# Spreading a global group's steps over other units, and moving the second merged pass, in a fused window-attention and feed-forward kernel

## The chip, the cores and the metric

The kernel runs on one core of a Trainium2 chip. The metric is the device time of one execution in microseconds. Its engines work side by side, each through its own instructions in order: TensorE (matmuls; PE in the profile, its weight loads PEld), VectorE (DVE), ScalarE (ACT), GpSimd (POOL) and SyncE (SP), which here only issues transfers.

## The reference

Eight batches with eight heads each. Every head has 512 local positions and 32 global ones, of 64 features. A local query attends to the 32 global keys and to local keys at most 32 positions away; a global query attends to all 544 keys. The result, 4608 rows of 512, goes through a feed-forward part: relu, square, scale and shift between two matrix products.

```python
s_g = scale * q_g @ k_all.T ; out_g = softmax(s_g) @ v_all
mask = abs(pos[:, None] - pos[None, :]) <= 32
s_l = concat([scale * q_l @ k_g.T, where(mask, scale * q_l @ k_l.T, -1e9)])
out_l = softmax(s_l) @ concat([v_g, v_l])
x = concat([out_g, out_l], axis=2)      # as (4608, 512)
r = maximum(x @ w_in, 0) ; out = (s * r * r + b) @ w_out
```

## The kernel before, in words

**Units and passes.** An attention unit j (0 to 127) is one head of one half (256 queries) of one batch: batch j // 16, half (j // 8) % 2, head j % 8. The feed-forward part has 17 tiles of 256 rows (the last holds the global rows), with eight passes m each, 136 in all; a pass multiplies one tile with a 256-wide slice of the first weights (`ffn_in`, 24 matmuls in the split precision that is used from pass 3 on), squares the result, and multiplies it with the matching slice of the second weights into two accumulators (`ffn_out`, twelve matmuls, six for each accumulator). Units 0 to 15 and passes 0 to 7 stand in a list written out by hand (PLAN). From pass 8 on the loop at the end (lines 753 to 826) puts one unit into each pass, from unit 16 on; in the passes of TWO_HEADS it puts two, here called merged passes: pass 10 holds units 18 and 19, pass 13 units 22 and 23. Unit 24 stands in pass 14, and from there on unit j in pass j - 10.

**The order.** For TensorE, ScalarE and VectorE the order of the program is the order of the engine's instructions (a manual schedule). SyncE's and GpSimd's order after the list is made by a planner. A usual pass goes: `split` of a unit two ahead (two casts on ScalarE, L236 and L238, and two subtractions on GpSimd, L237 and L239, which give keys and queries as a high and a low part); `begin`: the unit's score matmuls (L419, and L423 for the global queries) into the one score bank `ps_s` and the one bank `ps_g`, the masked scores with their maximum (`sm_scores`, VectorE L251), the global scores' copy (ScalarE L431) and addition (VectorE L437); `weigh`: two exponentials (L262), sums (L269, L270), two divides (L278); every fourth unit (j % 4 = 1) `values`: the value product of two pairs of units (L381), from the units j - 5 to j - 2, pair by pair; `ffn_in(m)`; `turned`: four copies into `two` (L458) and a transfer that transposes them (L464); on the last pass of a tile `x_split`, the cast of the next tile (L572) into the one buffer that `ffn_in` reads, and its low part (L576); `relu` (ScalarE L621); the joining of the unit before (`join`, ScalarE L472, which waits for the transposed data); `square` (VectorE L625); `g_high` (ScalarE L629) and `g_low` (VectorE L633); and last on TensorE `ffn_out(m - 1)`. After the last pass of a tile (in the pass behind it, called border in the code) two output copies follow on ScalarE (L660) with their transfers.

**Global groups.** A group (b, g) is the global queries of four heads of batch b. Its scores are complete after unit 16 b + 11 (g = 0) or 16 b + 15 (g = 1). Then come: its softmax (`g_softmax`, maximum on VectorE L480 and L481, exponential on ScalarE L486, sum and divide on VectorE L490 to L492), which stands at the end of a pass behind `g_low` (list `early`); copies of its five pieces into two 16-bit planes (`g_planes`, VectorE L529, list `planes_at`, behind `square`); a transposing transfer (L534); the joining of the pieces (`g_join`, ScalarE L541, list `joins_at`, behind the unit's `join`); the load of its values (`g_load`, L546); and its value product (`g_pv`, L554, list `gpv`, before `ffn_in`). Group 0 and 1 of batch 0 are transposed on TensorE instead (`g_turn`, L510, five matmuls, copied by `g_part`, L514). With s0 = 16 b + 12 + 4 g the softmax stands at unit s0, the planes at s0 + 1 (three) and s0 + 2 (two, with the transfer), the joinings at s0 + 3 (two pieces, and the load) and s0 + 4 (three), the value product at s0 + 5. Group (0, 1) has its softmax at unit 17 and its value product at unit 25.

**Splits ahead.** In a merged pass two units are split, so the loop makes up: the second unit's successor is split in the merged pass, and pass 17 (CATCH_UP) splits one more, from where on splits are two units ahead.

Of the kernel before, what the change touches and what calls it, by code (L numbers as in the profile page):

```python
# [22 lines left out]
P = 128  # L23
# [25 lines left out]
TWO_HEADS = (10, 13)  # L49
# [23 lines left out]
CATCH_UP = 17  # L73
# [8 lines left out]
def window_attention_then_ffn(ctx: ExitStack, tc: tile.TileContext, qd, qp, qg, kw, vw, vg, w_in, w_out, out):  # L82
# [433 lines left out]
    def g_transposes(b, g):  # L516
        for part in range(2):
            g_turn(b, g, part)
            g_part(b, g, part)
            yield  # L520

# [119 lines left out]
    def ffn_out(m, turn):  # L641
        t, pr = m // 8, m % 8
        g = gs_.pop(m)
        if pr == 0:
            oacc[t] = [ps.tile([P, DM], F32, tag=f"acc{i}", name=f"acc{t}_{i}") for i in range(2)]
        for i in range(2):
            next(turn, None)
            n = 0
            for k in range(2):
                f = 2 * pr + k  # L650
                for e, a in terms(m):
                    nc.tensor.matmul(  # L652
                        oacc[t][i], lhsT=as_used(m, g[:, a, k, i * P:(i + 1) * P]), rhs=weight(f, e)[:, 512:1024],
                        start=(pr == 0 and n == 0), stop=(pr == 7 and n == 5),
                    )
                    n += 1
        if pr == 7:
            for i in range(2):
# [22 lines left out]
    def run_max(j):  # L681
# [14 lines left out]
        "Fo": lambda m: ffn_out(m, iter(())),  # L696
# [16 lines left out]
    for b in range(B):  # L713
        for g in range(2):
            s0 = 16 * b + G_AT[g]
            first = int((b, g) == (0, 1))
            early[s0 + first].append(lambda b=b, g=g: g_softmax(b, g))
            if b < G_PE:
                turns[s0 + 3] = g_transposes(b, g)
                (joins_at if first else early)[s0 + 2 + 2 * first].append(lambda b=b, g=g: g_load(b, g))  # L720
            else:
                planes_at[s0 + 1].append(lambda b=b, g=g: g_planes(b, g, 0, 3))
                planes_at[s0 + 2].append(lambda b=b, g=g: (g_planes(b, g, 3, 5), g_turn_dma(b, g)))
                joins_at[s0 + 3].append(lambda b=b, g=g: (g_join(b, g, 0, 2), g_load(b, g)))
                joins_at[s0 + 4].append(lambda b=b, g=g: g_join(b, g, 2, 5))
            gpv[s0 + G_PV + 4 * first].append(lambda b=b, g=g: g_pv(b, g))
# [27 lines left out]
    for m in range(8, NM + 1):  # L754
# [7 lines left out]
        for i in heads:  # L762
            head_loads(i)
# [139 lines left out]
```

## Time and profile before

| | us |
|---|---|
| median of three runs | 969.67 (969.21 to 970.29) |
| the profiled execution | 969.21 |
| its span in the profile | 967.4 |
| TensorE busy in it | 934.8 (97%) |
| ScalarE, VectorE, GpSimd busy | 722.3, 664.3, 220.2 |

The span runs from the first instruction to the last. Busy time of TensorE counts matmuls from start to a modelled end, so a matmul that waits for its data between others can still count as busy; lost time is better seen in how long a stretch with known content takes. A row of the timeline gives start, duration, engine and line, and in brackets how long the engine had idled before and what ended that.

### The profile page before, as it was taken

The numbers are of one execution on the slowest core, as the hardware profiler recorded it, in microseconds if no ns is written. First come the engines' busy times: TensorE is split into PE (matmuls) and PEld (weight loads), VectorE is DVE, ScalarE is ACT, GpSimd is POOL, SyncE is SP. The second block draws the span as 40 slices with busy tenths as digits, with TensorE's granted clock in tenths as the row PEclk, the third lists the DMA queues.
The fourth block names the chain that finished last, engine by engine and source line by source line (L and its number), as shares of the span: only waits on it lengthen the run. The fifth ranks groups of instructions, "written<-read, shape, count | busy, mean of one in ns | idle before, by whom it ended". The sixth has DMA issues, their size and how long they took to land.

```text
span 967.4 us, 19993 instructions
## 1 busy us (share of the span) xinstructions
PE 934.8 (97%) x7258; PEld 832.1 (86%) x7258; DVE 664.3 (69%) x2058; ACT 722.3 (75%) x1514; POOL 220.2 (23%) x245
## 2 busy tenths in 40 slices
PE   7889899999999999999999999999999999999996
PEld 3658788898999989998999889998999999999995
DVE  5999777777768776776767676777768776752221
ACT  6999687788778887888778787878778887752321
POOL 1010233332333232323323232323323232100000
PEclk8999989999999999999999999999999999999999
DMA  9953344466455553466346554456345564232000
GB/s 318 384 190 100 104 110 104 127 141 143 112 111 143 126 135 95 121 144 152 86 116 141 123 138 97 116 144 163 84 110 143 140 126 106 62 72 73 22 1 23
DMA packets 195979, 119.68 MB, mean 124 GB/s; under 512 B 144168, under 2 KB 185128, under 8 KB 195880
## 3 DMA queue, kind: packets, MB, share of 16 engines
q1 hardware_dynamic: 190864, 109.28, 45.0%
q10 hardware_dynamic: 5016, 9.13, 2.7%
q8 instruction: 57, 0.93, 0.4%
q14 instruction: 42, 0.34, 0.1%
HBM read 74.98 MB, written 9.44 MB: 87 GB/s over the span
## 4 chain that ended last, share of the span: by engine, by line
PE 57%; DVE 18%; ACT 14%; DMA 5%; issue 4%; ACTq 1%; SPq 0%; POOL 0%; DVEq 0%; POOLq 0%
PE ps_h L613 25%; PE acc L652 23%; ACT sm L262 3%; PE ps_op L381 3%; DVE two L458 3%; PE ps_s L419 3%; DVE r L625 3%; DMA turned<-two 2%; DMA wst<-in_w_out 2%; ACT kq L236 2%; ACT g L629 2%; DVE wst L185 2%; ACT ptp L472 1%; DVE g L633 1%; DVE sm L278 1%
## 5 line engine op out<-in xcount | busy, mean ns | idle before, releaser
L613 PE MATMUL ps_h<-xs,wh 128*128 128x256 f32 x1584 | 288.8, 283 | 3.0 <-DVE r L625 2.8
L237 POOL TENSOR_TENSOR kq<-rk,kq 64x416 fp32r<-64x416 f32 x112 | 128.5, 1148 | 589.7 <-ACT kq L236 563.4
L652 PE MATMUL acc<-wh,g 128*128 128x512 f32 x792 | 249.1, 395 | 1.8 <-DVE g L633 1.4
L613 PEld LDWEIGHTS ps_h<-xs,wh 128*128 128x128 f32 x1584 | 243.5, 189 | 6.8 <-DVE r L625 2.9
L613 PE MATMUL ps_h<-xs,wl 128*128 128x256 f32 x792 | 220.0, 280 | 0.0
L633 DVE SCALAR_TENSOR_TENSOR g<-r,sb_t,g 128x512 fp32r<-128x512 f32 x133 | 100.5, 756 | 100.7 <-ACT g L629 100.7
L652 PEld LDWEIGHTS acc<-wh,g 128*128 128x128 f32 x792 | 142.8, 189 | 29.2 <-DVE g L633 3.0
L472 ACT COPY ptp<-turned 128x1024 int16<-128x1024 int16 x112 | 152.1, 1360 | 11.2 <-DMA turned<-two 11.0
L652 PE MATMUL acc<-wl,g 128*128 128x512 f32 x396 | 155.4, 392 | 0.0
L613 PEld LDWEIGHTS ps_h<-xs,wl 128*128 128x128 f32 x792 | 149.5, 189 | 0.1
L621 ACT ACTIVATE r<-ps_h 128x512 f32<-128x512 f32 x136 | 81.4, 599 | 89.4 <-PE ps_h L613 85.3
L625 DVE SCALAR_TENSOR_TENSOR r<-ps_h,sb_t,r 128x512 f32<-128x512 f32 x136 | 101.5, 747 | 56.4 <-ACT r L621 54.6
L629 ACT ACTIVATE g<-r,sb_t 128x512 fp32r<-128x512 f32 (+1 forms) x136 | 98.2, 722 | 50.8 <-DVE r L625 50.2
L262 ACT ACTIVATE sm<-sm,nm 128x224 f32<-128x224 f32 (+1 forms) x256 | 117.6, 461 | 6.2 <-DVE nm L251 4.6
L458 DVE COPY two<-sm 128x256 int16<-128x256 int16 x448 | 100.7, 288 | 8.7 <-DMA turned<-two 8.6
L613 PE MATMUL ps_h<-xs,w 128*128 128x256 f32 x816 | 102.8, 282 | 0.0
L652 PE MATMUL acc<-w,g 128*128 128x512 f32 x408 | 100.2, 393 | 0.2
L613 PEld LDWEIGHTS ps_h<-xs,w 128*128 128x128 f32 x816 | 98.1, 188 | 1.8
L652 PEld LDWEIGHTS acc<-wl,g 128*128 128x128 f32 x396 | 74.6, 188 | 16.6
L652 PEld LDWEIGHTS acc<-w,g 128*128 128x128 f32 x408 | 74.2, 188 | 15.8 <-DVE g L633 1.3
L239 POOL TENSOR_TENSOR kq<-rq,kq 128x256 fp32r<-128x256 f32 x112 | 83.9, 749 | 8.8
L419 PE MATMUL ps_s<-kq 128*128 128x192 f32 (+1 forms) x448 | 79.0, 266 | 5.3 <-POOL kq L237 5.1
(79 smaller groups left out, 1144.5 us busy)
## 6 DMA issues: line engine op xcount, KB each, us to landing
rvp<-in_vw SPq DMA_DIRECT2D x64, 256.0 KB
rq<-in_qd SPq DMA_DIRECT2D x112, 128.0 KB
rk<-in_kw SPq DMA_DIRECT2D x56, 208.0 KB
rvg<-in_vg SPq DMA_DIRECT2D x16, 640.0 KB
out<-o ACTq DMA_DIRECT2D x34, 256.0 KB
wst<-in_w_in SPq DMA_DIRECT2D x16, 512.0 KB
wst<-in_w_out SPq DMA_DIRECT2D x16, 512.0 KB
turned<-two SPq DMA_TRANSPOSE x112
```

The costliest lines, as they stand in the source:

```text
L237: nc.gpsimd.tensor_sub(out=ks[p1:p1 + 64], in0=rk[p0:p0 + 64], in1=f32(ks[p0:p0 + 64]))
L239: nc.gpsimd.tensor_sub(out=qs[:, 1, :], in0=rq, in1=f32(qs[:, 0, :]))
L262: nc.scalar.activation(out=p, in_=p, func=AF.Exp, bias=nm[:, n:n + 1], scale=-1.0, accum_out=ss[:, n:n + 1],)
L419: nc.tensor.matmul(p_s[:, cols], lhsT=qs[:, a, blk * P:(blk + 1) * P], rhs=ks[:, cols], start=(a == 0), stop=(a == 1),)
L458: nc.vector.tensor_copy(out=two[:, 2 * blk + c], in_=sm[:, :, c0:c0 + P])
L472: nc.scalar.copy(out=pt.bitcast(I16).rearrange("p c (q h) -> p c h q", h=2), in_=st_.pop(("turned", j)))
L613: nc.tensor.matmul(p_h[:, k], lhsT=weight(f, a)[:, c * P:(c + 1) * P], rhs=xcur[t][:, c, :] if m < PLAIN else xs_[t][:, e, c, :], start=(n ...
L621: nc.scalar.activation(out=r, in_=st_["ph", m], func=AF.Relu)
L625: nc.vector.scalar_tensor_tensor(out=r, in0=st_.pop(("ph", m)), scalar=s_t, in1=r, op0=ALU.mult, op1=ALU.mult)
L629: nc.scalar.activation(out=as_used(m, g[:, int(m < PLAIN)]), in_=st_["r", m], func=AF.Identity, bias=b_t)
L633: nc.vector.scalar_tensor_tensor(out=g[:, 1], in0=st_.pop(("r", m)), scalar=b_t, in1=f32(g[:, 0]), op0=ALU.add, op1=ALU.subtract,)
L652: nc.tensor.matmul(oacc[t][i], lhsT=as_used(m, g[:, a, k, i * P:(i + 1) * P]), rhs=weight(f, e)[:, 512:1024], start=(pr == 0 and n == 0), ...
```

## The change

The second merged pass becomes pass 12 (units 21 and 22) instead of 13. In a merged pass the second unit's score matmuls stand between the two halves of `ffn_out` instead of in front of it, their evaluation on VectorE behind the first unit's `turned`, `square` and the planes, and the first unit's value product (`values`) keeps its usual place. The splits that make up stand in passes 9, 11 and 17, behind the joinings. The softmax of group g = 0 goes to unit 16 b + 11 (from 16 b + 12), that of g = 1 to unit 16 b + 17 (from 16 b + 16), except in the last batch. The planes follow it (two pieces, then three with the transfer). For g = 0 the first joining goes from unit 16 b + 15 to 16 b + 14, with the load; the second stays. For g = 1 one joining of all five pieces at 16 b + 21 takes the place of those at 16 b + 19 and 16 b + 20; the load goes from 16 b + 19 to 16 b + 20, and the value product from 16 b + 21 to 16 b + 25. The transposes on TensorE of batch 0 stand behind `ffn_out` instead of ahead of its two halves.

```diff
-TWO_HEADS = (10, 13)
+TWO_HEADS = (10, 12)
...
-CATCH_UP = 17
+AHEAD = (9, 11, 17)
...
-    def ffn_out(m, turn):
+    def ffn_half(m, i):
         t, pr = m // 8, m % 8
-        g = gs_.pop(m)
-        if pr == 0:
-            oacc[t] = [ps.tile([P, DM], F32, tag=f"acc{i}", name=f"acc{t}_{i}") for i in range(2)]
-        for i in range(2):
-            next(turn, None)
-            n = 0
...
+        g = gs_[m]
+        if pr == 0 and i == 0:
+            oacc[t] = [ps.tile([P, DM], F32, tag=f"acc{k}", name=f"acc{t}_{k}") for k in range(2)]
+        n = 0
...
+    def ffn_sent(m):
...
+    def ffn_out(m):
+        for i in range(2):
+            ffn_half(m, i)
+        ffn_sent(m)
...
-            first = int((b, g) == (0, 1))
-            early[s0 + first].append(lambda b=b, g=g: g_softmax(b, g))
-            if b < G_PE:
-                turns[s0 + 3] = g_transposes(b, g)
-                (joins_at if first else early)[s0 + 2 + 2 * first].append(lambda b=b, g=g: g_load(b, g))
+            pe, late = b < G_PE, g == 1 and b < B - 1
+            e0 = s0 + (0 if b == B - 1 and g else 1 if g else -1)
+            early[e0].append(lambda b=b, g=g: g_softmax(b, g))
+            if pe:
+                turns[s0 + 3] = lambda b=b, g=g: [fn(b, g, i) for i in range(2) for fn in (g_turn, g_part)]
+                joins_at[s0 + (4 if late else 2)].append(lambda b=b, g=g: g_load(b, g))
             else:
-                planes_at[s0 + 1].append(lambda b=b, g=g: g_planes(b, g, 0, 3))
-                planes_at[s0 + 2].append(lambda b=b, g=g: (g_planes(b, g, 3, 5), g_turn_dma(b, g)))
-                joins_at[s0 + 3].append(lambda b=b, g=g: (g_join(b, g, 0, 2), g_load(b, g)))
-                joins_at[s0 + 4].append(lambda b=b, g=g: g_join(b, g, 2, 5))
-            gpv[s0 + G_PV + 4 * first].append(lambda b=b, g=g: g_pv(b, g))
+                planes_at[e0 + 1].append(lambda b=b, g=g: g_planes(b, g, 0, 2))
+                planes_at[e0 + 2].append(lambda b=b, g=g: (g_planes(b, g, 2, 5), g_turn_dma(b, g)))
+                joins_at[e0 + 3].append(lambda b=b, g=g: g_load(b, g))
+                for j, c0, c1 in ((s0 + 5, 0, 5),) if late else ((e0 + 3, 0, 2), (s0 + 4, 2, 5)):
+                    joins_at[j].append(lambda b=b, g=g, c0=c0, c1=c1: g_join(b, g, c0, c1))
+            gpv[s0 + (9 if late else 5)].append(lambda b=b, g=g: g_pv(b, g))
...
             begin(a)
             weigh(a)
-        if z > a:
-            split(cut)
-            cut += 1
-        elif m == CATCH_UP:
-            split(cut)
-            cut += 1
-        if z == a:
-            values(a)
+        values(a)
         if m < NM:
             ffn_in(m)
-            if z > a:
-                begin(z)
+        if z:
+            ffn_half(m - 1, 0)
+            products(z)
...
             relu(m)
-            join_before(a)
-            at(joins_at, a)
+        join_before(a)
+        at(joins_at, a)
+        if m in AHEAD:
+            split(cut)
+            cut += 1
+        if z:
+            g_copy(z)
...
             square(m)
-            at(planes_at, a)
+        at(planes_at, a)
...
+        if z:
+            sm_scores([z], [st_.pop(("ps1", z))])
+            g_add(z)
+        if m < NM:
             g_high(m)
             g_low(m)
...
-        if z > a:
+        if z:
             weigh(z)
             turned(z)
-            at(joins_at, z)
-            at(planes_at, z)
-            at(early, z)
-        turn_g = [turns.pop(i) for i in heads if i in turns]
-        ffn_out(m - 1, turn_g[0] if turn_g else iter(()))
...
+            ffn_half(m - 1, 1)
+            ffn_sent(m - 1)
+        else:
+            ffn_out(m - 1)
         if border:
             at(early, a)
-        if z > a:
-            values(z)
+        for i in heads:
+            if i in turns:
+                turns.pop(i)()
```

## Rows read from the trace of the kernel before

**Rows 1.** The page, part 1: TensorE's busy time and share, its weight loads, other engines

```profile
PE 934.8 (97%) x7258; PEld 832.1 (86%) x7258; DVE 664.3 (69%) x2058; ACT 722.3 (75%) x1514; POOL 220.2 (23%) x245
```

**Rows 2.** Stretches from unit to unit, early: length, busy times, clock, transfers' share, GB/s

```profile
112.53:128.16 15.63, 10.36 (x54) 8.64 (x52) 12.30 (x36) 11.09 (x25) 4.15 (x5) 0.78 0.39 102
128.16:134.24 6.08, 6.08 (x43) 5.59 (x42) 4.87 (x22) 5.56 (x12) 2.16 (x2) 1.00 0.46 108
142.11:148.98 6.87, 6.87 (x51) 6.39 (x49) 5.34 (x20) 5.07 (x13) 3.73 (x4) 1.00 0.27 76
155.09:165.82 10.73, 9.24 (x115) 7.95 (x114) 8.14 (x26) 9.54 (x19) 1.90 (x2) 1.00 0.63 147
178.04:184.87 6.83, 6.54 (x44) 5.70 (x42) 5.52 (x20) 5.44 (x11) 2.61 (x3) 1.00 0.40 96
```

**Rows 3.** Sum of six stretches, r = 1 to 5 of six batches, same view

```profile
sum 220.86, PE 218.04 PEld 195.52 DVE 157.26 ACT 187.35 POOL 56.22; mean PE 36.34 PEld 32.59 DVE 26.21 ACT 31.23 POOL 9.37
```

**Rows 4.** Five clean steps, r = 1 to 5: the last one, and their sum

```profile
562.89:571.48 8.59, 8.59 (x116) 7.78 (x115) 5.76 (x20) 7.75 (x16) 1.81 (x2) 1.00 0.68 175
sum 35.51, PE 35.51 PEld 32.46 DVE 25.37 ACT 29.63 POOL 9.36; mean PE 7.10 PEld 6.49 DVE 5.07 ACT 5.93 POOL 1.87
```

**Rows 5.** Timeline of the first merged pass

```profile
119.59 0.54 ACT L236 CAST kq<-rk 64x416 fp32r<-64x416 f32 x1
...
121.11 0.42 DVE L437 TENSOR_TENSOR sg<-ps_g,tg 32x256 f32<-32x256 f32 x1
...
121.47 0.53 PE L419 MATMUL ps_s<-kq 128*128 128x192 f32 x1 [5.12 <-POOL kq L237]
...
122.48 1.37 DVE L278 TENSOR_SCALAR sm<-sm,ss 128x192 f32<-128x192 f32 x2
```

**Rows 6.** Stretches in and behind TensorE's wait there: the clock is third from the end

```profile
116.35:120.00 3.65, 0.00 (x1) 0.00 (x0) 1.86 (x6) 1.97 (x4) 0.00 (x0) 0.98 0.38 72
120.00:126.50 6.50, 4.96 (x16) 3.93 (x17) 5.95 (x20) 4.65 (x12) 3.84 (x4) 0.50 0.26 73
```

**Rows 7.** Timeline of batch 2, r = 11 to 13, around the first group's softmax

```profile
285.99 1.23 SPq L464 DMA_TRANSPOSE turned<-two  x1
...
287.29 0.52 ACT L236 CAST kq<-rk 64x416 fp32r<-64x416 f32 x1
...
290.19 0.57 DVE L278 TENSOR_SCALAR sm<-sm,ss 128x224 f32<-128x224 f32 x2
...
290.42 1.37 ACT L472 COPY ptp<-turned 128x1024 int16<-128x1024 int16 x1 [0.27 <-DMA turned<-two]
...
292.26 0.72 ACT L629 ACTIVATE g<-r,sb_t 128x512 fp32r<-128x512 f32 x1 [0.47 <-DVE r L625]
...
292.33 1.66 PE L381 MATMUL ps_op<-ptp,rvp 128*64 128x128 f32 x32
...
295.49 0.54 ACT L236 CAST kq<-rk 64x416 fp32r<-64x416 f32 x1
```

**Rows 8.** Timeline of batch 3, r = 1 to 4, behind the second group's softmax

```profile
324.20 1.16 ACT L572 CAST xs<-x 128x512 fp32r<-128x512 f32 x2
...
327.51 0.72 ACT L629 ACTIVATE g<-r,sb_t 128x512 fp32r<-128x512 f32 x1 [0.41 <-DVE r L625]
...
339.79 0.79 ACT L541 COPY pg<-pg 128x512 int16<-128x512 int16 x1
...
339.89 0.75 DVE L625 SCALAR_TENSOR_TENSOR r<-ps_h,sb_t,r 128x512 f32<-128x512 f32 x1
...
341.43 0.75 DVE L633 SCALAR_TENSOR_TENSOR g<-r,sb_t,g 128x512 fp32r<-128x512 f32 x1 [0.79 <-ACT g L629]
...
342.15 0.63 PE L652 MATMUL acc<-wh,g 128*128 128x512 f32 x2
```

**Rows 9.** Timeline of batch 4, r = 15 and 0: a transpose behind the load

```profile
419.63 1.23 SPq L464 DMA_TRANSPOSE turned<-two  x1
...
424.23 1.37 ACT L472 COPY ptp<-turned 128x1024 int16<-128x1024 int16 x1 [0.99 <-DMA turned<-two]
```

More of the change, by code (lines that the diff above doesn't have):

```diff
@@ L514, in g_part @@
         nc.scalar.copy(out=st_["pg", b, g][:, c0:c1], in_=st_["ptg", b, g, part][:, 0:c1 - c0])
[L516 to L520, printed above, removed]
     def g_planes(b, g, c0, c1):
@@ L639, in window_attention_then_ffn @@
     oacc = {}
-    def ffn_out(m, turn):
+    def ffn_half(m, i):
         t, pr = m // 8, m % 8
-        g = gs_.pop(m)
-        if pr == 0:
-            oacc[t] = [ps.tile([P, DM], F32, tag=f"acc{i}", name=f"acc{t}_{i}") for i in range(2)]
-        for i in range(2):
-            next(turn, None)
-            n = 0
[L649 to L657, printed above, removed]
+        g = gs_[m]
+        if pr == 0 and i == 0:
+            oacc[t] = [ps.tile([P, DM], F32, tag=f"acc{k}", name=f"acc{t}_{k}") for k in range(2)]
+        n = 0
+        for k in range(2):
+            f = 2 * pr + k
+            for e, a in terms(m):
+                nc.tensor.matmul(
+                    oacc[t][i], lhsT=as_used(m, g[:, a, k, i * P:(i + 1) * P]), rhs=weight(f, e)[:, 512:1024],
+                    start=(pr == 0 and n == 0), stop=(pr == 7 and n == 5),
+                )
+                n += 1
+    def ffn_sent(m):
+        t = m // 8
+        if m % 8 == 7:
             for i in range(2):
@@ L756, in window_attention_then_ffn @@
         j = heads[-1] + 1
-        a, z = heads[0], heads[-1]
+        a, z = heads[0], heads[1] if len(heads) > 1 else None
         border = (m - 1) % 8 == 7
@@ L761, in window_attention_then_ffn @@
                 load(i + 3)
-        for i in heads:
             head_loads(i)
@@ L806, in window_attention_then_ffn @@
                 xg_split(16)
-        else:
-            join_before(a)
-            at(joins_at, a)
-            at(planes_at, a)
         if not border:
             at(early, a)
-        if z > a:
+        if z:
             weigh(z)
             turned(z)
-            at(joins_at, z)
-            at(planes_at, z)
-            at(early, z)
-        turn_g = [turns.pop(i) for i in heads if i in turns]
-        ffn_out(m - 1, turn_g[0] if turn_g else iter(()))
+            for hooks in (joins_at, planes_at, early, gpv):
+                assert z not in hooks
+            ffn_half(m - 1, 1)
+            ffn_sent(m - 1)
+        else:
+            ffn_out(m - 1)
         if border:
             at(early, a)
-        if z > a:
-            values(z)
+        for i in heads:
+            if i in turns:
+                turns.pop(i)()
     assert all(k < NF for d in (early, gpv, turns, joins_at, planes_at) for k in d)
```

4 lines of the change are left out of this document (3 added, 1 removed).

## The prediction

> **What bounds the kernel now.** The page comes first: TensorE is busy 97% of the span [rows 1], so a change can only win what is left in single places. A busy matmul may still be a late one, so I read TensorE by stretches next, cut where the global-score matmul of one unit starts and that of the next one does. A clean pass with one unit is 6.1 us (the stretch from 128.16) [rows 2]; a merged pass adds one set of score matmuls, and the second merged pass (units 22 and 23) shows that at 6.87 it loses nothing [rows 2]. Three stretches early on are too long. The first merged pass (units 18 and 19, with five transposes of a global group) takes 15.63 where 6.87 and the transposes would do: some 8 lost. Unit 25's step takes 10.73 where one with the same content takes 8.59 [rows 2, 4]: 2.1 lost. Unit 28's takes 6.83: 0.7 lost. After that I call r the number of a unit modulo 16. In six batches the five steps r = 1 to 5, where a second global group is worked off, sum to 220.86 us [rows 3]; five clean ones are 35.51 [rows 4], six times that 213.06, so 7.8 us are lost there. Everything else runs at the clean length. The places to look at are therefore the merged pass and the steps around the global groups.
>
> **Why those places lose.** In the merged pass TensorE waits 5.12 us for GpSimd's half of unit 19's keys, because ScalarE reaches that unit's cast only at 119.59 us [rows 5], behind the softmax of global group (0,1). The clock is at 0.98 over the idle 3.65 us and at 0.50 in the 6.5 us behind it, that is 1.2 instead of 2.4 GHz [rows 6]. In the later batches ScalarE and VectorE walk behind TensorE: a pass's square waits for relu and the copies, the high part of g for the square, the low part for the high one, and the next pass's output matmuls for that. In batch 3's r = 3 the low part ends at 341.43 + 0.75 = 342.18, where TensorE wanted it from 342.15 [rows 8]: there the slack is used up to the last tenth.
>
> **The change, part by part.**
>
> *First merged pass.* Unit 19's casts move to the pass before, into about a microsecond in which ScalarE waits anyway. The wait for GpSimd goes. What is late next is VectorE: there is one score bank, so unit 19's scores can't start before VectorE has read unit 18's, and it does that behind the same softmax, ending with the addition at 121.11 + 0.42 = 121.53 [rows 5]. The matmuls thus begin at 121.1, only 0.4 us earlier than at 121.47. Behind them, unit 20's scores need VectorE's divides, copies, square, and scores and addition of 18 and of 19: the same instructions that fill 5.95 of the 6.5 us from 120.00 to 126.50 [rows 6], now in another order. So unit 20's third score matmul starts at 125.6 to 126.4 instead of 128.16 (the edge in rows 2). I take 2.2 us won. Ends: 0.3 if TensorE's clock falls again (of the 4.8 us from its last matmul at 116.35 to 121.1 half an output now fills some 1.5, so no single wait reaches the 3.65 after which it fell, and I take full speed); 8 if no wait is left.
>
> Two divides took 1.37 us at 122.48 [rows 5] with GpSimd subtracting beside them, and 0.57 at 290.19 [rows 7]. The Trainium skill (SBUF — State Buffer, Who interferes with whom) states that VectorE in a two-port mode and GpSimd exclude each other for a whole instruction; by it each moved subtraction may add up to 0.8 us once, so the part would give 1.4 instead of 2.2. That stays inside the ends above.
>
> *Second merged pass* a pass earlier, with unit 21's value product in it. Its work is the same; between the second scores and the next unit's stand half an output (a quarter of a clean pass, 1.5 us) instead of a whole one. I charge 0.3 us of new waits on the one score bank (0 to 1.5). In exchange unit 23 stands alone two passes before unit 25 wants its joining, as in every later batch where that position is clean: the 2.1 of unit 25 go (0 to 2.1). Unit 28's 0.7 goes too: the extra cast of its predecessor now stands behind relu (0 to 0.7).
>
> *First group's softmax (g = 0) from r = 12 to r = 11*, seven times. Where it stands now, ScalarE's next cast starts at 295.49, though the high part of g ended at 292.26 + 0.72; without a softmax the cast starts right at its end (287.29) [rows 7]. So a softmax holds the next unit back by 2.6 us. Today the next step is r = 13, which carries a value product and hides it. From r = 11 it falls on r = 12: its relu, which ended 0.27 before 290.42, ends at some 292.7, and the joining behind it takes 1.37 to 294.1. The value product of r = 13 starts at 292.33, and the second of its two halves, 0.83 later at 293.15, reads exactly that joining [rows 7]. TensorE waits 0.95 us: 6.6 in seven batches. Ends: 0 if ScalarE makes it up, 1.3 if all 2.6 arrive at the joining (which lost 0.27 to a transfer before). Nothing behind it gains, as TensorE then runs at its clean length anyway.
>
> *Second group's softmax (g = 1) from r = 0 to r = 1*, six times. Leaving r = 0 gives little: in r = 1 the cast of the new tile can't start before TensorE is through with the old one, and it starts at 324.20 already; that and 0.41 of waiting before the high part are what ScalarE can make up, some 0.7 of 2.6 us. The rest, 1.9, falls on r = 2, a step with two output copies and no value product, and runs on into r = 3, where there is no slack: the output matmuls of 342.15 wait 1.9 us [rows 8], partly one step earlier. Six times: 11.4 (ends 0 and 2.6 each).
>
> *Planes and joinings.* The two joinings leave r = 3 and r = 4. In r = 3 the joining (339.79 + 0.79 = 340.58) ended before the square (339.89 + 0.75 = 340.64) for which the high part waited [rows 8]: worth nothing there. In r = 4 the second (three pieces, so some 1.2 us at 0.79 for two) is in front of nothing late any more. The whole joining in r = 5, at most 2.5 times 0.79 = 2.0 us, lies under that step's value product. The planes' copies stand beside ScalarE's high part as before: 0. The group's value product goes from r = 5 to r = 9, both of one length: 0. The 7.8 us lost there today, part of them waits for a transfer as at 424.23 [rows 9], are replaced by the 11.4.
>
> *Transfers.* The value load of a group goes one step earlier (g = 0) or later (g = 1), and on SyncE's queue the unit's transpose stands behind it. Behind the load a transpose is issued at 419.63 and joined at 424.23, 4.6 us [rows 9]; without a load it is issued at 285.99 and lands at 290.42, 4.4 us [rows 7]. So I charge 0. The loads of a merged pass only change places among themselves: 0.
>
> The Trainium skill (DMA: Bandwidth & Descriptors, Queues, rings and completion order) states that each DMA engine takes descriptors in ring order; by it the transpose would wait for all of the load. The two rows show 0.2 us of it.
>
> **Sum.** -2.2 + 0.3 - 2.1 - 0.7 = -4.7 early; +6.6 for g = 0; 11.4 - 7.8 = +3.6 for g = 1: +5.5. The profiled execution took 969.21 us (span 967.4), which gives 974.7; the median of the three runs is 0.46 higher, and I forecast 975.2.
>
> **Rivals.**
> 1. *The joinings were the brake* (faster). Place: r = 3 and r = 4, ScalarE. If the lag there is ended by the 0.79 and 1.2 us of joining and not by the square, the lateness carried out of r = 1 is cancelled and the 11.4 fall to about 0: 975.2 - 11.4 = 963.8. It decides from the point where the high part of g in r = 3 follows a joining. Against it: 340.58 before 340.64; for it: a margin of 0.06 us.
> 2. *The merged pass closes altogether*: 8 instead of 2.2, so 969.4, no change. It asks that VectorE read unit 18's scores before 120; nothing in the change puts them ahead of the softmax.
> 3. *The load does hold the transpose back*, in r = 5 with the whole joining behind it: a wait of up to 1.1 us in six batches, 981.8.
> 4. *The change does nothing to the merged pass*, if unit 19's keys are loaded too late to be cast ahead: 977.4. Unit 19 shares its keys with 18, so I hold it unlikely.
>
> **Chances.** Forecast 0.55, rival 1 0.22, rival 2 0.12, rivals 3 and 4 together 0.11. The forecast's own range is 970.5 to 979.5, from the ends of the g = 0 and g = 1 terms. The range given, 963.5 to 980, takes in rival 1. What a measurement of this kernel can tell from no change is about 0.2%, 1.9 us. Of the forecast 0.05 is within that: faster 0.24, same 0.15, slower 0.61.
>
> **What would show it.** Right: no 5 us wait of the scores for GpSimd; unit 20's global scores near 126; steps r = 13 near 8.8 instead of 7.9, with the value product waiting for a joining; r = 3 and r = 4 together longer by nearly 2 us in every batch, also in those clean today; unit 25 at 8.6. Wrong: r = 13 still at 7.9, or r = 4 at 6.1, which would mean that ScalarE takes up the softmax somewhere that I don't see; or a first merged pass under 9 us.

## The result and the profile after

The changed kernel takes 975.26 us (median of four runs, 974.04 to 976.79); the kernel before, beside it, 969.98 (969.21 to 970.44). The ratio is 1.006, with a 95% interval of 1.0047 to 1.0073: slower by 0.6%. The forecast was 975.2. The profiled execution took 974.04 with a span of 972.3; before it was 969.21 and 967.4.

The page's first part, the same row as in [rows 1], shows that no engine has more instructions. TensorE's modelled busy time is 2.6 us longer and the span 4.9, so the difference is waiting and not work:

```profile
PE 937.4 (96%) x7258; PEld 830.9 (85%) x7258; DVE 659.1 (68%) x2058; ACT 723.4 (74%) x1508; POOL 221.7 (23%) x245
```

Where it is shows in stretches from one unit's global-score matmul to the next, as in [rows 2]. First the early part of the changed kernel: units 18 and 19 (now 13.11, before 15.63), 20, 21 and 22, 24, 25, and 28. Columns: length, busy time of TensorE, its weight loads, VectorE, ScalarE, GpSimd, granted clock, transfers' share, GB/s.

```profile
111.77:124.88 13.11, 8.93 (x54) 6.79 (x52) 10.75 (x36) 10.75 (x22) 4.72 (x5) 1.00 0.41 111
124.88:131.04 6.16, 6.16 (x41) 5.65 (x42) 4.94 (x21) 6.04 (x16) 2.06 (x2) 1.00 0.55 119
131.04:139.48 8.44, 8.44 (x80) 7.63 (x79) 6.69 (x24) 8.11 (x19) 3.95 (x4) 1.00 0.65 168
145.81:152.70 6.89, 6.60 (x44) 5.68 (x42) 4.73 (x18) 6.49 (x12) 1.82 (x2) 1.00 0.39 90
152.70:161.26 8.56, 8.56 (x116) 7.74 (x114) 6.77 (x21) 6.81 (x16) 1.91 (x2) 1.00 0.66 158
173.48:179.71 6.23, 6.23 (x43) 5.56 (x42) 4.18 (x14) 4.40 (x12) 3.63 (x4) 1.00 0.45 103
```

The first merged pass gains 2.52, unit 25 gains 2.17 (10.73 before), unit 28 0.60 (6.83). Units 21 to 24 together take 21.66 (131.04 to 152.70) where they took 20.85 (134.24 to 155.09 in [rows 2]): 0.81 given back, nearly all of it in unit 24. With 0.08 for unit 20 the early part is 4.40 shorter.

The same view gives the two places that pay. The first row is r = 13 of batch 2, 7.90 long before; then the sum over its seven batches; the last two rows are the sums of r = 3 and 4, and of r = 1 to 5, over batches 2 to 7.

```profile
289.16:298.07 8.91, 8.29 (x75) 7.37 (x74) 7.62 (x29) 7.67 (x16) 2.41 (x3) 1.00 0.63 143
...
sum 62.44, PE 58.05 PEld 51.59 DVE 53.39 ACT 53.71 POOL 16.85; mean PE 8.29 PEld 7.37 DVE 7.63 ACT 7.67 POOL 2.41
...
sum 84.21, PE 80.02 PEld 67.88 DVE 62.34 ACT 68.56 POOL 22.32; mean PE 13.34 PEld 11.31 DVE 10.39 ACT 11.43 POOL 3.72
...
sum 219.69, PE 215.50 PEld 191.22 DVE 151.19 ACT 169.51 POOL 56.30; mean PE 35.92 PEld 31.87 DVE 25.20 ACT 28.25 POOL 9.38
```

The same seven steps took 55.27 before, so 7.17 more. The five steps r = 1 to 5 took 220.86 [rows 3]: 1.17 less now. But the group's value product has left r = 5 for r = 9, which grows from 47.36 to 51.47 over the six batches (4.11), so that group costs 2.9 more, and r = 6 another 0.2. Balance: -4.40 + 7.17 + 3.15 = +5.9. The span differs by 4.9, because unit 16 happened to start 0.76 earlier in this execution (98.67 against 99.43), where the two programs are still alike (over all profiled runs of this study that start lies between 98.7 and 101.1), and what stands behind unit 127's start took 0.3 less.

**The merged pass.** The timeline of the changed kernel answers to [rows 5]. A row gives start, duration, engine, line, operation and tiles; the brackets hold how long the engine had idled and what ended that.

```profile
118.00 0.75 ACT L486 ACTIVATE sg<-sg,gm 128x544 f32<-128x544 f32 x1 [1.64 <-DVE gm L481]
119.26 0.50 DVE L492 TENSOR_SCALAR sg<-sg,gs 128x544 f32<-128x544 f32 x1
119.68 0.35 DVE L251 CUSTOM_DVE_ANT_0 sm<-ps_s,mask 128x192 f32<-128x192 f32 x1
120.49 0.33 PE L419 MATMUL ps_s<-kq 128*128 128x192 f32 x1 [1.87 <-DVE nm L251]
124.52 0.33 PE L419 MATMUL ps_s<-kq 128*128 128x192 f32 x1 [1.06 <-DVE nm L251]
```

The 5.12 us wait for GpSimd is gone. What is late next is what the prediction named: VectorE reads unit 18's scores only at 119.68, behind the softmax of group (0,1), and unit 19's scores wait 1.87 us for that. The clock stays at 1.00 (0.50 in [rows 6]). That holds for this execution only: in seven of the runs below with the same pass (e2, e3, e4, e8, e10, e11, e13) the granted clock is 0.50 (1.2 instead of 2.4 GHz) for 3.41 us behind the same wait of 1.9 us. Units 18, 19 and 20 together are at most 0.13 longer there than here.

**r = 13**, against [rows 7]. The softmax now stands ahead of r = 12's work:

```profile
286.22 0.75 ACT L486 ACTIVATE sg<-sg,gm 128x544 f32<-128x544 f32 x1 [1.64 <-DVE gm L481]
286.97 0.52 ACT L236 CAST kq<-rk 64x416 fp32r<-64x416 f32 x1
289.86 1.33 ACT L472 COPY ptp<-turned 128x1024 int16<-128x1024 int16 x1
289.47 1.15 PE L381 MATMUL ps_op<-ptp,rvp 128*64 128x128 f32 x18
291.24 0.93 PE L381 MATMUL ps_op<-ptp,rvp 128*64 128x128 f32 x14 [0.62 <-ACT ptp L472]
```

The value product took 1.66 us in one piece [rows 7]; now it is cut in two, waiting for the joining that ends at 289.86 + 1.33 = 291.19. From 289.47 to 292.17 it takes 2.70: 1.04 more.

**r = 3 and 4** of batch 3, against [rows 8]. The softmax's cast delay (1.64 us of waiting for the maximum) carries to the output matmuls of r = 4, a step that was clean in this batch before:

```profile
327.24 0.75 ACT L486 ACTIVATE sg<-sg,gm 128x544 f32<-128x544 f32 x1 [1.64 <-DVE gm L481]
341.41 0.50 PE L644 MATMUL acc<-wh,g 128*128 128x512 f32 x1 [0.34 <-ACT g L623]
342.20 0.50 PE L644 MATMUL acc<-wh,g 128*128 128x512 f32 x1 [0.28 <-DVE g L627]
```

r = 3 is 6.7 and r = 4 is 7.3 in each of the six batches, where 6.1 is clean. The modelled ends show 0.6 of that as idle time; the length of the step shows all of it.

### The profile page after: what moved, and what is told of

Read it like the earlier page. It is cut to its first block, busy times and chain, and to the rows that moved or that the text cites. A ratio compares the mean times of both kernels' runs of the same rounds, so it can differ in the third digit from the quotient of the medians.

```text
span 972.3 us, 20000 instructions
## 1 busy us (share of the span) xinstructions
PE 937.4 (96%) x7258; PEld 830.9 (85%) x7258; DVE 659.1 (68%) x2058; ACT 723.4 (74%) x1508; POOL 221.7 (23%) x245
## 3 DMA queue, kind: packets, MB, share of 16 engines
q10 hardware_dynamic: 5016, 9.13, 2.6%
## 4 chain that ended last, share of the span: by engine, by line
PE 59%; DVE 18%; ACT 15%; issue 4%; DMA 2%; ACTq 1%; SPq 0%; DVEq 0%
PE ps_h L607 26%; PE acc L644 24%; PE ps_op L381 4%; ACT sm L262 3%; PE ps_s L419 3%; ACT ptp L472 2%; DVE r L619 2%; DVE two L458 2%; DVE g L627 2%; ACT g L623 2%; DVE wst L185 2%; ACT o L655 2%; DVE we L191 1%; DMA wst<-in_w_out 1%; ACT xs L566 1%
```

## The experiments

Twelve kernels ran, each beside the kernel before on its chip. The table gives the median, its ratio to before with the 95% interval, and from each trace the length of units 18 + 19, the mean of r = 13, and the lengths of r = 3 and r = 4 in batches 2 to 7 (one number where all agree within 0.1, else the extremes).

| kernel | us | ratio | 18 + 19 | r = 13 | r = 3 | r = 4 |
|---|---|---|---|---|---|---|
| before | 969.98 | | 15.63 | 7.90 | 6.1 | 6.09 to 7.10 |
| changed | 975.26 | 1.006 | 13.11 | 8.92 | 6.7 | 7.3 |
| e1_g0_back | 968.76 | 0.9999 (0.9989 to 1.0009) | 13.06 | 7.90 | 6.7 to 6.9 | 7.3 |
| e2_g1_back | 965.37 | 0.9965 (0.9954 to 0.9976) | 13.07 | 8.93 | 6.1 | 6.06 to 6.26 |
| e3_both_back | 964.68 | 0.9948 (0.9928 to 0.9969) | 13.16 | 7.90 | 6.1 | 6.09 to 7.14 |
| e4_only_merged | 964.1 | 0.9945 (0.9928 to 0.9962) | 13.17 | 7.90 | 6.1 | 6.12 to 7.13 |
| e5_only_groups | 980.6 | 1.0118 (1.0099 to 1.0136) | 15.84 | 8.93 | 6.7 | 7.3 |
| e6_split_softmax | 959.93 | 0.9902 (0.9887 to 0.9916) | 12.14 | 7.90 | 6.1 | 6.4 to 6.5 |
| e8_idle_copies | 975.88 | 1.0067 (1.0052 to 1.0083) | 13.09 | 8.93 | 6.7 | 7.3 |
| e9_split_01 | 976.03 | 1.0068 (1.0054 to 1.0081) | 12.21 | 8.93 | 6.7 | 7.3 |
| e10_merged_13 | 976.34 | 1.0076 (1.0064 to 1.0088) | 13.07 | 8.93 | 6.7 | 7.3 |
| e11_split_first | 958.5 | 0.9899 (0.9885 to 0.9913) | 13.16 | 7.90 | 6.1 | 6.10 to 6.24 |
| e13_load_later | 960.77 | 0.9917 (0.9905 to 0.9929) | 13.18 | 7.90 | 6.1 | 6.08 to 6.38 |
| e14_together | 958.56 | 0.9891 (0.9876 to 0.9906) | 12.10 | 7.90 | 6.1 | 6.1 |

**1. The first groups put back (e1).**

```diff
-            e0 = s0 + (0 if b == B - 1 and g else 1 if g else -1)
+            e0 = s0 + (1 if g and b < B - 1 else 0)
```

> The changed kernel with only the first groups' (g = 0) softmax, planes, joinings and load put back to their old units (r = 12 to 15, 0); all else as changed. Theory (the softmax at r = 11 makes r = 12's relu and joining late, and the value product of r = 13 waits for it): the steps r = 13 go from 8.9 back to 7.9 us in seven batches, 7 us in all, so about 968.2 us. Rival (the longer r = 13 comes from something else that the change moved, such as ScalarE's order of split and joining): r = 13 stays at 8.9 and the time at 975. If ScalarE makes part of it up, r = 13 lands between.

968.76, and r = 13 is 7.90 in all seven batches. The theory (968.2) holds. r = 3 and r = 4 don't change, but for one step (6.86 in batch 5).

**2. The second groups put back (e2).**

```diff
-            e0 = s0 + (0 if b == B - 1 and g else 1 if g else -1)
+            e0 = s0 + ((1 if b == 0 else 0) if g else -1)
```

> The changed kernel with only the second groups' (g = 1) softmax put back to r = 0 and the planes to r = 1 and 2 (batches 1 to 6), the load with them; the joining stays whole in r = 5 and the value product in r = 9. Theory (the softmax at r = 1 falls on r = 2 to 4, where there is no slack): r = 3 goes from 6.7 to 6.1 and r = 4 from 7.3 to 6.1, so 1.8 us in six batches, 10.8 in all: about 964.5. Had the kernel before lost its 7.8 us in r = 1 to 5 to the softmax at r = 0 and not to the joinings, r = 4 would come back only to the 6.9 to 7.1 that it had there in four batches: some 7 won, 968. Rival (the softmax's place is indifferent, the whole joining in r = 5 or the value product in r = 9 costs the time): r = 3 and r = 4 stay, 975.

965.37. The sum of r = 3 and r = 4 over six batches, the row that was 84.21 above, with all of TensorE's time busy:

```profile
sum 73.51, PE 73.51 PEld 67.47 DVE 48.77 ACT 57.88 POOL 22.34; mean PE 12.25 PEld 11.24 DVE 8.13 ACT 9.65 POOL 3.72
```

10.7 us come back, as the theory said; batch 5 loses 0.6 of them again in r = 5 (8.50 for 7.9). But r = 4 is clean in batches where it was 6.9 to 7.1 before, although the softmax stands at r = 0 as it did then. What differs from before in these steps is the second groups' chain behind the softmax (the cut of the planes, the joinings, the value product), and the first groups' chain, one step earlier. The next runs part the two.

**3. The groups' new places alone (e5).** The kernel before with the new lines for softmax, planes, joinings, load and value product:

```diff
-            first = int((b, g) == (0, 1))
-            early[s0 + first].append(lambda b=b, g=g: g_softmax(b, g))
...
+            e0 = s0 + (0 if b == B - 1 and g else 1 if g else -1)
+            early[e0].append(lambda b=b, g=g: g_softmax(b, g))
...
```

> The kernel before with only the new places of the groups' softmax, planes, joinings, loads and value products; the merged passes and splits as before. Theory (the two parts add up): the early gain of some 5 us is missing and the cost of the groups' new places stands alone: before's 969.7 plus 7.1 (r = 13) plus 2.6 (r = 1 to 5 and r = 9) = 979.5. Rival (the losses in the later batches come from the new order of the passes, such as the split's place, not from the groups): within 1 us of before, and r = 13, 3 and 4 as before.

980.6, with r = 13, 3 and 4 as in the changed kernel. The theory holds: the groups' new places cost 11.7 us by themselves. The two parts add up only roughly: with the 4.8 that the merged passes win alone (run 6) they make +6.9, where the changed kernel shows +5.3. Part of that is unit 28, which takes 7.60 here, 6.83 before and 6.23 in the changed kernel.

**4. The joinings' load put back (e8).**

```diff
+            if late and not pe:
+                joins_at[s0 + 3].append(lambda: g_idle(2))
+                joins_at[s0 + 4].append(lambda: g_idle(3))
...
+    def g_idle(n):
+        nothing = sb.tile([P, 256], I16, tag="nothing", name="nothing", bufs=1)
+        for i in range(n):
+            nc.scalar.copy(out=nothing, in_=f32(high[8]).bitcast(I16)[:, 0:256])
```

> The changed kernel with copies on ScalarE that nobody reads put where the second groups' joinings stood before: two in r = 3, three in r = 4, in batches 1 to 6 (about the time that the joinings took). Theory (the joinings cost nothing beside the square in r = 3, and r = 4 has slack behind the wait): the time rises by under 2 us. Rival (ScalarE's work in r = 3 and 4 is itself the brake, so each copy is paid in full): 0.8 + 1.2 = 2 us in six batches, 12 us more, 987.

975.88, and not one of r = 3 and r = 4 is longer by more than 0.02. The 30 copies took 0.405 us each, 12.2 in all, and cost nothing that can be measured: work on ScalarE at the joinings' old places is no brake. Rival 1 falls.

**5. Both put back (e3).**

```diff
-            e0 = s0 + (0 if b == B - 1 and g else 1 if g else -1)
+            e0 = s0 + (1 if b == 0 and g else 0)
```

> The changed kernel with the softmax and planes of both kinds of groups put back to their old units (r = 12 and r = 0); the new merged passes, the whole joining in r = 5 and the value product in r = 9 of the second groups stay. Theory (the two costs are independent and add up): 975.3 - 7.1 - 10.8 = 957.5, against before that is 1.2% faster. Rival (each of the two hides a part of the other, so that the second one undone brings less): 960 to 963.

964.68, 7 us over the theory, and over the rival too (the seven runs spread from 961.3 to 968.5; the trace is of one with 962.8). r = 13 and r = 3 are clean, but r = 4 is near 7 in four batches again, and r = 2 in two, with no joining in r = 3 and r = 4. So neither the joinings nor the second groups' softmax alone makes that loss. It came back with the *first* groups' chain, the only thing that differs from run 2.

**6. The merged passes alone (e4).** The changed kernel with the groups' lines of before:

```diff
-            e0 = s0 + (0 if b == B - 1 and g else 1 if g else -1)
-            early[e0].append(lambda b=b, g=g: g_softmax(b, g))
...
+            first = int((b, g) == (0, 1))
+            early[s0 + first].append(lambda b=b, g=g: g_softmax(b, g))
...
+                joins_at[s0 + 3].append(lambda b=b, g=g: (g_join(b, g, 0, 2), g_load(b, g)))
+                joins_at[s0 + 4].append(lambda b=b, g=g: g_join(b, g, 2, 5))
...
```

> The changed kernel with the groups' places wholly as before (softmax r = 12 and r = 0, joinings of the second groups in r = 3 and r = 4, value product in r = 5); only the merged passes, the splits and the half outputs are new. Theory: the early gain alone, 4.7 less than before, about 964.5, with the later batches losing their 7.8 us in r = 1 to 5 as before. Rival (the new splits' places alone repair r = 1 to 5, not the moved joinings): r = 4 and r = 5 clean, about 957.

964.1: the early gain stands by itself, 4.8 us (before was 968.89 in this set). r = 1 to 5 take 219.2, hardly less than before (220.9), so the rival falls.

**What the loss of before was.** The steps r = 4 of batches 2 to 7 of the kernel before, as stretches, in the order of the columns above:

```profile
231.66:238.60 6.94, 6.66 (x44) 5.68 (x42) 5.50 (x21) 6.49 (x14) 2.24 (x3) 1.00 0.69 193
338.87:344.98 6.11, 6.11 (x44) 5.66 (x42) 4.58 (x17) 5.12 (x11) 1.91 (x2) 1.00 0.82 210
446.24:453.30 7.06, 6.67 (x44) 5.65 (x42) 5.31 (x19) 6.04 (x14) 2.33 (x3) 1.00 0.65 197
555.78:562.88 7.10, 6.67 (x43) 5.68 (x42) 5.50 (x21) 6.78 (x15) 2.38 (x3) 1.00 0.74 203
663.88:670.91 7.03, 6.65 (x43) 5.69 (x42) 5.50 (x21) 6.84 (x15) 2.32 (x3) 1.00 0.64 192
771.14:777.23 6.09, 6.09 (x44) 5.62 (x42) 4.56 (x17) 5.09 (x11) 1.89 (x2) 1.00 0.88 211
```

And these are all the waits of ScalarE for transposed data in r = 0 of those batches, some 22 us earlier, from the timeline; the one in batch 4 (0.99 us, at 424.23) stands in [rows 9]:

```profile
209.53 1.37 ACT L472 COPY ptp<-turned 128x1024 int16<-128x1024 int16 x1 [0.26 <-DMA turned<-two]
...
533.84 1.37 ACT L472 COPY ptp<-turned 128x1024 int16<-128x1024 int16 x1 [2.20 <-DMA turned<-two]
...
641.86 1.38 ACT L472 COPY ptp<-turned 128x1024 int16<-128x1024 int16 x1 [1.56 <-DMA turned<-two]
```

Batches 2, 4, 5 and 6 wait in r = 0 and lose in r = 4; batches 3 and 7 do neither. In batch 5, where the wait is longest, r = 2 loses too (7.10). These waits don't go with all of the 7.8 us: r = 1, 2 and 4 lose 5.8 together, and r = 5 loses 2.1 in batches 3, 4 and 7, where ScalarE waits 1.6, 1.7 and 0.9 us for transposed data in r = 4, behind the second groups' load. SyncE's queue of the kernel before shows what stands ahead of 533.84's transpose:

```profile
525.85 0.33 SPq L546 DMA_DIRECT2D rvg<-in_vg  x1
526.27 0.38 SPq L226 DMA_DIRECT2D rq<-in_qd  x1
526.74 0.98 SPq L399 DMA_DIRECT2D rqg<-in_qg  x1
527.82 1.26 SPq L464 DMA_TRANSPOSE turned<-two  x1
```

Three loads, 640 + 128 + 129 KB by the profile's list of issues, stand within 2 us ahead of the transpose, and it lands 6.02 us after its issue, where one without a load took 4.4 [rows 7]. The Trainium skill (DMA: Bandwidth & Descriptors, Queues, rings and completion order) states that each DMA engine takes descriptors in ring order; this row agrees. But the same three loads, the first 1.37 us ahead, stand there in batches 2, 3, 4 and 6 as well, where the data was taken 4.3, 4.3 (without a wait), 4.6 and 6.0 us after the issue; what makes these differ is open. In the changed kernel the group's load stands a step earlier, apart from the other one of 129 KB (520.10 and 526.13), and ScalarE doesn't wait in r = 0 in any batch. Two runs on the kernel with both softmaxes back test it.

**7. The load later (e13).**

```diff
-    def g_load(b, g):
+    def g_load(b, g, queue=nc.sync):
...
-                joins_at[e0 + 3].append(lambda b=b, g=g: g_load(b, g))
+                joins_at[e0 + 3 if g else s0 + 4].append(lambda b=b, g=g: g_load(b, g, nc.sync if g else nc.scalar))
```

> The kernel of the run with both softmaxes put back (964.7 us; r = 2 and r = 4 together 5.6 us over clean), with one thing changed: the value load of the first groups (640 KB), there issued by SyncE in r = 15 ahead of the transpose of that unit, is issued by ScalarE in r = 0 instead, behind the joining of that unit's data. Theory (what the later batches lose around r = 2 and r = 4, before as well, starts with ScalarE's wait for that transpose, up to 1.8 us here, behind the loads): the wait in r = 0 goes, the low part of r = 0 ends 7.6 us behind the step's start in every batch, r = 2 and r = 4 are clean, about 959; if the load then comes too late for the value product of r = 1, that step shows it. Rival (the softmaxes' own lag, carried from the first group's to the second's, is the cause): r = 4 stays near 7 in four batches, 964 to 966.

960.77. The wait is gone, r = 2 is clean, and r = 4 all but once (6.38): the load does hold the transpose back. The edit moves it in time and to another queue at once, and which of the two counts is not parted. The same place of batch 5, the load on ScalarE's queue, the other on SyncE's, and the joining 4.46 behind the transpose's issue with no wait before it:

```profile
525.08 0.36 ACTq L540 DMA_DIRECT2D rvg<-in_vg  x1
525.57 1.35 ACT L472 COPY ptp<-turned 128x1024 int16<-128x1024 int16 x1
...
521.11 1.23 SPq L464 DMA_TRANSPOSE turned<-two  x1
```

r = 1 is longer in two batches (8.84 and 9.28 for 8.6), where the load comes late for its own value product. r = 5, which is not in the table, is longer in two (8.65 and 8.36 for 7.9), with waits of ScalarE of 1.5 us for transposed data in r = 4. The waits of TensorE in r = 1 of batch 7 are one row:

```profile
PE ps_og L548 <- DMA rvg<-in_vg: 0.6, 1, 0.6
```

**8. The first groups' softmax cut (e11).**

```diff
-            early[e0].append(lambda b=b, g=g: g_softmax(b, g))
+            if g:
+                early[e0].append(lambda b=b, g=g: g_softmax(b, g))
+            else:
+                planes_at[e0].append(lambda b=b, g=g: g_max(b, g))
+                early[e0].append(lambda b=b, g=g: g_exp(b, g))
+                planes_at[e0 + 1].append(lambda b=b, g=g: g_divide(b, g))
```

> The kernel of the run with both softmaxes put back (964.7 us), with only the first groups' softmax (r = 12) cut in three, the load where it was (r = 15). Rival of the load theory (the lag that the first group's softmax leaves on ScalarE is carried into the second's): r = 2 and r = 4 clean, about 959. Theory (the transpose behind the load is the cause, whatever the softmax does): the wait of r = 0 for the transposed data stays, r = 4 stays near 7 in about four batches, 963 to 965.

958.5: the rival's number, with the load left where it was. The theory of the load alone fails. The trace joins the two:

```profile
525.26 1.35 ACT L472 COPY ptp<-turned 128x1024 int16<-128x1024 int16 x1
...
518.36 0.33 SPq L540 DMA_DIRECT2D rvg<-in_vg  x1
518.78 0.38 SPq L399 DMA_DIRECT2D rqg<-in_qg  x1
519.63 1.72 SPq L464 DMA_TRANSPOSE turned<-two  x1
```

The transpose still stands behind both loads, and its data is joined 5.63 us after the issue, without a wait. In the run that this one starts from (e3) the same place shows:

```profile
527.38 1.38 ACT L472 COPY ptp<-turned 128x1024 int16<-128x1024 int16 x1 [1.80 <-DMA turned<-two]
```

There the transpose is issued 0.49 us before the step r = 0 begins (521.04 against 521.53). Here, with no lag left by the softmax, VectorE has the copies ready sooner, and it is issued 1.68 before (519.63 against 521.31). These 1.19 us alone don't cover the wait of 1.80: the transpose also lands 4.9 us after its issue, against 6.3 in e3, behind the same two loads, and why it is quicker is not shown. The loss in r = 2 and r = 4 ends when either the load ahead of the transpose (e13) or the lag of the first groups' softmax (e11) is taken away.

r = 5 is not clean. It takes 8.04, 9.13 and 9.13 in batches 3 to 5 where 7.9 is clean, 2.6 us in all, with waits of ScalarE of 0.9, 1.95 and 2.0 us for transposed data in r = 4, behind the second groups' load.

**9. Every softmax cut, in its new place (e6).** On the changed kernel, for all groups:

```diff
-            early[e0].append(lambda b=b, g=g: g_softmax(b, g))
+            planes_at[e0].append(lambda b=b, g=g: g_max(b, g))
+            early[e0].append(lambda b=b, g=g: g_exp(b, g))
+            planes_at[e0 + 1].append(lambda b=b, g=g: g_divide(b, g))
```

> The changed kernel with each group's softmax still in its new unit but cut in three: the maximum behind that unit's square, ahead of ScalarE's wait for it; the exponential where the softmax stood; the sum and divide behind the next unit's square. Theory (what costs is ScalarE's wait for VectorE's maximum behind the low part, some 1.6 of the 2.6 us that a softmax holds it back; the exponential itself is under 1 us): r = 13 goes to 7.9 or nearly, r = 3 to 6.1 and r = 4 to at most 6.4, so 975.3 - 7 - 9 to 10.8 = 957 to 960. Rival (the place alone decides, any softmax work there is paid): r = 3, 4 and 13 stay within 0.3 of the changed kernel, 970 to 975.

959.93, 15 us under the changed kernel without moving a group. r = 13 and r = 3 are clean, r = 4 keeps 0.3. ScalarE in r = 11 of batch 2, to compare with the 286.22 above:

```profile
283.28 0.72 ACT L623 ACTIVATE g<-r,sb_t 128x512 fp32r<-128x512 f32 x1 [0.71 <-DVE r L619]
284.09 0.75 ACT L486 ACTIVATE sg<-sg,gm 128x544 f32<-128x544 f32 x1
```

The exponential follows the high part at once. Of the 2.6 us that a softmax held ScalarE, 1.64 were the wait for a maximum that VectorE only began behind the low part. So a softmax costs what it does in the new units because it stands there uncut, and not by the unit alone. The cut moves the sum and the divide too; what the earlier maximum is worth by itself is not parted from that.

**10. Only the softmax ahead of the merged pass cut (e9).** The same three lines, under a condition:

```diff
+            if (b, g) != (0, 1):
+                early[e0].append(lambda b=b, g=g: g_softmax(b, g))
+            else:
...
```

> The changed kernel with the softmax of group (0,1) alone, the one ahead of the first merged pass, cut in three in the same way. Theory (what is late in that pass is VectorE's reading of unit 18's scores behind the softmax, with one score bank): units 18 and 19 together get shorter by 1 to 2 us from 13.1, about 973.7 in all. Rival (the pass is limited elsewhere, by the half outputs' own order or by the clock): within 0.3 us of the changed kernel.

976.03, no change. Units 18 and 19 do get 0.9 shorter (12.21), so VectorE's reading behind the softmax did limit that pass. The next wait in it is then the group's transposes on TensorE, for the divide that the cut had moved behind unit 18's square:

```profile
124.96 0.77 PE L510 MATMUL ps_tg<-ident,sg 128*128 128x128 f32 x5 [1.98 <-DVE sg L492]
```

And units 21 and 22 take 9.29 in place of 8.44, which gives 0.85 of the 0.9 back. The rows of TensorE's weight loads show where: 0.45 is in the value product, of which one weight load waits 0.27 for a joining, and 0.4 at unit 23's scores, where one load waits 0.37 for nothing that the profile names and the next 0.20 for VectorE's addition. What makes these late is left open.

**11. The second merged pass put back to pass 13 (e10).**

```diff
-TWO_HEADS = (10, 12)
+TWO_HEADS = (10, 13)
...
-AHEAD = (9, 11, 17)
+AHEAD = (9, 12, 17)
```

> The changed kernel with the second merged pass put back to pass 13 (units 22 and 23; splits that make up in passes 9, 12 and 17), all else as changed. Theory (it is the place of that pass that took unit 25's 2.1 us and brought the new wait of 0.8 in unit 24): unit 25 goes back from 8.6 towards 10.7, unit 24's wait goes, so 1 to 1.5 us more than the changed kernel, 976.5. Rival (the new order inside the pass, not its place, took unit 25's loss): unit 25 stays at 8.6 and the time at 974.5 to 975.3.

976.34. Unit 24 is 6.16 again, so its new wait is the place's; unit 25 takes 9.69, half way between 8.56 and 10.73. The place and the new order inside the pass, with its splits, each took about half of unit 25's loss; the groups' new places have no part in it (10.69 in e5).

**12. Together (e14).** Everything cut, old units, the second groups' load as in the changed kernel.

```diff
+            e0 = s0 + (1 if b == 0 and g else 0)
+            planes_at[e0].append(lambda b=b, g=g: g_max(b, g))
+            early[e0].append(lambda b=b, g=g: g_exp(b, g))
+            planes_at[e0 + 1].append(lambda b=b, g=g: g_divide(b, g))
...
+                joins_at[s0 + (4 if late else 3)].append(lambda b=b, g=g: g_load(b, g))
```

> The new merged passes, the softmaxes and planes of both kinds of groups in their old units but all cut in three, the joinings and value product of the second groups as in the changed kernel, and their value load in r = 4 as there (not r = 3 as in the run with the first groups' softmax cut, 958.5, where r = 5 lost 1.2 us in two batches behind waits of 2 us for a transpose in r = 4). Theory (each of these losses is a transpose that comes too late, behind a load or behind the lag of a softmax): r = 1 to 5 clean in every batch, 955 to 957. Rival (the load moved to r = 4 brings the same wait one step later, in r = 5, where it costs as much): 958 to 960.

958.56: with e11 the fastest, 1.1% under before, and not to be told from e11. r = 1 to 4 are clean in all batches and r = 5 loses 0.2 and 0.5 in two, so r = 1 to 5 win 2.1 us over e11 by the traces. In r = 4 of those two batches ScalarE still waits 1.4 and 1.6 us for a transpose. The first of the two places:

```profile
334.18 0.33 SPq L540 DMA_DIRECT2D rvg<-in_vg  x1
335.59 1.23 SPq L464 DMA_TRANSPOSE turned<-two  x1
340.95 1.36 ACT L472 COPY ptp<-turned 128x1024 int16<-128x1024 int16 x1 [1.39 <-DMA turned<-two]
```

The load that was to stand a step later has not moved against the transpose: SyncE's order is the planner's, and it is issued 1.4 and 1.6 us ahead of these two, as in e11 (1.7 and 1.6). So this run tries neither the theory nor the rival on that load, and the time is the rival's without its reason.

And unit 20 takes 7.68 for 6.1, as in e6 (7.50), where the cut softmax of group (0,1) stands too. TensorE is busy all through it, but its granted clock (third from the end) is down:

```profile
125.19:128.60 3.41, 3.38 (x17) 3.32 (x17) 3.31 (x11) 2.39 (x7) 1.53 (x2) 0.50 0.03 8
```

3.41 us at 1.2 instead of 2.4 GHz are 1.7 us of full speed lost, in e6 as here. Ahead of it TensorE had waited 1.91 us for the divide in both; in e9 it waited 1.98 and the clock stayed at 1.00. Why it fell in two of the three is left open.

## Why the prediction was right

The time came out at 975.26 for 975.2, and the mechanisms at the three large places are those forecast. That the two agree within 0.1 us is luck: the terms are off by up to 0.7 and partly cancel, and the traces sum to +5.9 where +5.5 was forecast. Term by term, from the profiled execution:

- *First merged pass*: 2.5 won, 2.2 forecast. The wait for GpSimd went, VectorE's reading behind the softmax was next (shown by e9), and the clock stayed up. The reason given for the clock does not hold: no single wait would reach the 3.65 us after which it had fallen, yet in seven other runs it fell behind waits of 1.9 us. It cost at most 0.13 there; the wait of 1.06 us that TensorE has in that pass here (at 124.52) takes it up.
- *Second merged pass*: 0.8 of new waits, 0.3 forecast, and the resource was wrong. The one score bank is not what is late: unit 23's copies wait 0.94 for the one buffer `two`, which the transpose of unit 22 is still reading, since that unit's copies took long beside GpSimd's subtractions (below). That the wait goes with the place is shown (e10); that the slow copies start it was read from the trace and not tried.
- *Units 25 and 28*: 2.17 and 0.60 won, 2.1 and 0.7 forecast. The reason given for unit 25, the place, was half of it (e10).
- *First groups*: 7.2 lost, 6.6 forecast: 1.02 in each r = 13 for 0.95, by a value product waiting for a joining. Shown by e1, and by e6, where the lag is taken away in place.
- *Second groups*: 10.7 for 11.4 in r = 3 and r = 4, shown by e2. r = 2, where the prediction had the lag begin, stayed clean on TensorE (6.1); r = 3 loses 0.6 and r = 4 1.2, together the "nearly 2 us" that it named.
- *Planes and joinings, 0*: right. e8 put their load back for nothing. Rival 1, which got 0.22, had no ground: the 0.06 us between joining and square that spoke for it was no brake.
- *The 7.8 us lost before*: that the change replaces them was right, but the prediction gave no reason for it, and the cause was mostly wrong. It put them on ScalarE's and VectorE's lag in r = 1 to 5, "part of" them on a transfer. e11 and e13 take away the 5.6 that e3 loses in r = 2 and r = 4, and so show that this begins in r = 0, with the transpose; the kernel before has the same waits there and loses 5.8 in r = 1, 2 and 4. Its other 2.1, in r = 5, go with a like wait in r = 4, and no run tried that one.
- *Transfers, 0*: this is the step that failed, though it cost the total nothing. One transpose behind the load took 4.6 us [rows 9], and I charged the 0.2 between that and 4.4 as if all six batches were like it. At the next such place it took 6.02, with a wait of 2.2. It didn't spoil the sum, because in the changed kernel no wait is left in r = 0. Where it comes back beside the late softmax, in e1 (up to 2.2 us), r = 1 to 5 together are only 0.5 longer than in the changed kernel.

## What to carry to other kernels

Before a block of work is moved off a crowded step, look at what it holds up and for whom: here the engine stood for 1.64 of 2.6 us waiting for a maximum, and cutting the block in three won 15 us (e6 against the changed kernel) where the groups' new places alone had lost 11.7 (e5 against before). A loss that appears in some repetitions of a pattern and not in others is worth a row per repetition: the list of r = 4 beside the list of waits in r = 0 led to a cause that one row had hidden. After moving an issue in the program, look where the queue has it: in e14 a load stood where it had been. And two gains that are each shown alone may not add: putting back the first groups won 6.5 us and the second groups 9.9, both together 10.6, because the first groups' old place brings back the late transpose.

## What was not expected of the hardware

Four copies on VectorE that usually take 0.9 us together (e.g. 0.89 for the four at 122.23 of this trace) took 2.33 in the second merged pass, where GpSimd's two subtractions ran beside them. The timeline of the changed kernel:

```profile
140.98 2.33 DVE L458 COPY two<-sm 128x256 int16<-128x256 int16 x4
143.38 1.23 SPq L464 DMA_TRANSPOSE turned<-two  x1
...
140.95 1.26 POOL L237 TENSOR_TENSOR kq<-rk,kq 64x416 fp32r<-64x416 f32 x1 [4.41 <-DMA turned<-two]
142.29 0.87 POOL L239 TENSOR_TENSOR kq<-rq,kq 128x256 fp32r<-128x256 f32 x1
...
146.57 0.91 DVE L458 COPY two<-sm 128x256 int16<-128x256 int16 x4 [0.94 <-DMA turned<-two]
```

The Trainium skill (SBUF — State Buffer, Who interferes with whom) states that VectorE in a two-port mode and GpSimd exclude each other for a whole instruction, and the trace agrees: of the four copies one took 1.18 and one 0.82, each ending 0.15 us behind the subtraction beside it. The prediction had allowed for it in the first merged pass, where two divides took 0.57 as ever; it came in the second, and at 1.4 us instead of 0.8. Nor was it foreseen how far one transfer's time can spread. Counting only places where ScalarE stood waiting for it, the same transpose, of the same size, had its data taken between 3.7 us (e3, the joining at 556.33 with a wait of 0.75) and 7.0 us (e5, the joining at 249.25 with a wait of 1.82) after its issue. Both stand behind a group's load, so a load ahead does not by itself say how long it takes.
